# A transformer block in split fp32: mixing rebuilt in source order and overlapped with its neighbours, the MLP's first token block prepared inside it, masks as products in the scores' own type

## The chip, the cores and the metric

The kernel runs on one core of one Trainium2 chip. The metric is device microseconds of one launch, as a median over runs. Engines are named as in the profile: PE multiplies, PEld loads its weights, DVE, ACT and POOL work on vectors, SP issues the DMAs. Of the kernel before there are three runs: 1945.34, 1952.02 and 1945.75 us, median 1945.75.

## The reference

One sequence of S = 2048 tokens with D = 576 features, all fp32. `mod` is a vector of six modulations computed from a condition.

```
# attention: 32 heads of 18, causal window of 256
scores = where((0 <= i-j < 256), q @ k.T * 18**-0.5, -1e9);  o = softmax(scores) @ v
x = x + ga * (o @ wo)
h = layernorm(x) * (1 + cb) + sb
# mixing: four quarters of the features are shifted by +1, -1, +2, -2 tokens
u = gelu(layernorm(h) @ w1)
h1 = h + shift(u) @ w2
# MLP, F = 4608
out = x + gb * (h1 + gelu(layernorm(h1) @ w3) @ w4)
```

## The kernel before

**Arithmetic.** Each fp32 matrix is held as a high part in fp32r (a rounded fp32 that PE takes) and a low part, the rest. A product runs as three matmuls per 128 features: high·high, low·high, high·low. 576 features are four chunks of 128 and a tail of 64; the tail is stored twice in one chunk of 128 rows, high over low, so that one matmul makes two of its products. ACT casts the high part, DVE or POOL subtracts to get the low part. The w3 product is done by a Strassen scheme with seven products of half-size blocks (`OP`, `up` names P1 to P7); its operands on the activations' side are seven sums of quarter blocks, `A` (A11, A12, S3, ...), on the weights' side seven sums T1 to T4 and B11 to B22 of a slab of w3, `W`.

**Stages.** (1) `qkv`. (2) `attention`: 32 steps n, each of two head pairs j. Per j, four pairs of score blocks (`mx`, L522) of 64 queries against 320 keys, twice each, get the mask added by a second matmul with `identb` as weights and the mask `Mq` as moving operand (L524, or L526 where only one edge lies in the block). DVE takes row maxima (L534). Then the transposed scores X are computed in five banks of 512 columns (L566), with the masks `Mk` added by further matmuls (L591, nine per j), and ACT takes the exponential (L596). `identb`, `Mq` and `Mk` are bf16, the scores fp32r. Then P·V (L618), normalisation and a store of o to DRAM (`od`). Output tiles `wotile`: load o rows (`or`), transpose (`pa`, `pb`, L682/L684), split into T (L691 and before), 2 × 14 matmuls with Wo (L703), residual and layernorms, stores of x, h and the normalised h (`xp`, `hbd`, `xnd`). Tiles 12 to 15 run after the last heads.

(3) Mixing, `phase_b`: 8 groups of 256 tokens. Load `xnd`, transpose (L1055/L1057), split into T (L912/L913); five w1 chains per group (`pg`, L957, 14 matmuls of 256 columns, the last with the tail's 64 rows); gelu; high and low of the result into G (L961/L962, the tail chunk by quarters in L974/L975); small DVE copies carry the halo of one or two tokens between groups (L967 to L983), one right behind each chain's G; then per tile two chains with w2 (`w`, L1010, 14 matmuls of 288 columns). POOL makes `rr` = gb·h1 + x (L1020, L1021); SP stores it (`rd`) and the normalised h1 (`xmd`). w1 and w2 are loaded and split just before (`load_w1`, `load_w2`).

(4) MLP, `phase_m`: two token blocks of 1024, each 18 steps. Step jj uses slab j of w3 (256 of the 4608 columns) and w4. `wprep` loads a slab into the one buffer `wf` (L1089, L1090), sums on POOL (L1101), casts on ACT (L1107), splits on POOL (L1113) and DVE (the tail, L1121); for w4 POOL multiplies by gb (L1127) and splits (L1139). `up` is 7 × 7 matmuls of 512 columns (u0P, u1P, ..., L1211), combined, gelu, split into G (L1241); `down` is 16 × 6 matmuls of 288 (d, L1264), added by DVE to `acc` (L1272), which starts from `rd`. The A operands of a token block are made by `aprep`: load `xmd` into `rows` (L1159, L1160; the same buffer as `wf`), sums on POOL (L1167 to L1172), 84 transposes (L1182, L1183), splits (L1190 to L1192). The downs of step jj run between the products of step jj + 1, except around a block's end: there the last two downs run side by side with `aprep` of the next block.

**What sets the order.** `phase_a` (stages 1 and 2) collects events with hand-written nominal times (`tm(h)`, 11.5 a step) and plays them sorted. `phase_b` and `phase_m` play their own lists through a heap (`play`, `spread`), phase_b under the framework's own scheduling, phase_m in written order. Each has its own SBUF pools and PSUM pool; a pool's space passes to the next when the pool closes. Within an engine instructions run strictly in order.

Of the kernel before, what the change touches and what calls it, by code (L numbers as in the profile page):

```python
# [32 lines left out]
def spread(steps, t0, t1):  # L33
    n = len(steps)
    return [(t0 + (t1 - t0) * (k + 0.5) / n, f) for k, f in enumerate(steps)]


def play(timed):
    heap = [(t, n, f) for n, (t, f) in enumerate(timed)]
    heapq.heapify(heap)  # L40
    n = len(heap)
    while heap:
        f = heapq.heappop(heap)[2]
        for t, e in f() or ():
            heapq.heappush(heap, (t, n, e))
            n += 1


class Kern:
# [8 lines left out]
    def pool(self, stack, name, bufs=1, space=None):  # L58
        kw = {} if space is None else {"space": space}
        return stack.enter_context(self.tc.tile_pool(name=name, bufs=bufs, **kw))  # L60

    def split9(self, row, L, cs, name):
        nc = self.nc
        pa = self.ps.tile([P, KC, P], F32, tag="tr", name=name + "pa", bufs=self.b_tr)
        for k in range(KC):
            nc.tensor.transpose(pa[:, k, :], row[:, k * P:(k + 1) * P], self.ident)
        nc.scalar.copy(L[:, 0:KC, cs], pa)
        nc.vector.tensor_tensor(out=L[:, KC:2 * KC, cs], in0=pa, in1=L[:, 0:KC, cs].bitcast(F32), op=ALU.subtract)
        pb = self.ps.tile([TAIL, P], F32, tag="tr", name=name + "pb", bufs=self.b_tr)
        nc.tensor.transpose(pb, row[:, KC * P:D], self.ident)  # L70
        nc.scalar.copy(L[:TAIL, 2 * KC, cs], pb)
        nc.vector.tensor_tensor(out=L[TAIL:, 2 * KC, cs], in0=pb, in1=L[:TAIL, 2 * KC, cs].bitcast(F32), op=ALU.subtract)

    def passes(self, hi, lo):
        p = []
        for k in range(KC):
            p += [(hi[:, k, :], (slice(None), k)), (hi[:, k, :], (slice(None), KC + k)), (lo[:, k, :], (slice(None), k))]
        p.append((hi[:, KC, :], (slice(None), 2 * KC)))
        p.append((lo[:TAIL, KC, :], (slice(0, TAIL), 2 * KC)))
        return p  # L80

    def load_dup(self, raw, src):
        self.nc.sync.dma_start(raw[:TAIL], src)
        self.nc.sync.dma_start(raw[TAIL:], src)

    def stats(self, x, name):
        nc, sm = self.nc, self.sm
        st = sm.tile([P, 2, 6], F32, tag="bst", name=name + "st", bufs=3)
        mv = sm.tile([P, 2], F32, tag="bmv", name=name + "mv", bufs=4)
        rs = sm.tile([P, 1], F32, tag="brs", name=name + "rs", bufs=4)  # L90
        nc.vector.bn_stats(st[:, 0], x[:, 0:288])
        nc.vector.bn_stats(st[:, 1], x[:, 288:576])
        nc.vector.bn_aggr(mv, st)
        nc.gpsimd.tensor_scalar(rs, mv[:, 1:2], EPS, None, op0=ALU.add)
        nc.gpsimd.tensor_tensor(out=rs, in0=rs, in1=self.mhalf, op=ALU.pow)
        return mv[:, 0:1], rs

    def modulate(self, h, x, m, rs, scale_b, shift_b, way):
        nc = self.nc
        if way == "p":  # L100
            nc.vector.tensor_scalar(h, x, m, rs, op0=ALU.subtract, op1=ALU.mult)
            nc.gpsimd.tensor_tensor(out=h, in0=h, in1=scale_b, op=ALU.mult)
            nc.gpsimd.tensor_tensor(out=h, in0=h, in1=shift_b, op=ALU.add)
            return
# [60 lines left out]
    def masks(self):  # L165
        nc = self.nc
        g = nc.gpsimd
        for M in (self.Mq, self.Mk):
            g.memset(M, 0.0)
# [1182 lines left out]
```

## Time and profile before

| what | value |
|---|---|
| median of 3 runs | 1945.75 us |
| profiled execution | 1945.12 us |
| its span in the trace | 1943.1 us |
| mean granted clock of PE | 0.950 |
| instructions | 34458 |
| PE busy | 1763.9 us, 91% of the span |
| DVE / POOL / ACT busy | 1129.3 / 881.8 / 703.0 us |

The span runs from the first to the last instruction in the trace. Stages by the trace: qkv to about 230, attention to about 745, the last output tiles to 790, mixing to 959, the MLP from there (u0 first at 1014.5), its second token block from about 1437. Groups in the profile are named by line, engine and operation, `out<-in`, shapes, count; then busy time, mean ns of one, and the idle time of the engine just before them with what ended it.

### The profile page before, as it was taken

To read this page: it belongs to the slowest core of one execution; us is meant where nothing else is said; L and a number is where in the kernel's file an instruction comes from. 1 tells how busy PE (TensorE), PEld (TensorE's weight loads), DVE (VectorE), ACT (ScalarE), POOL (GpSimd) and SP (SyncE) were. 2 spreads that over 40 slices of the span, in tenths; PEclk is the share of its full clock that TensorE was granted. 3 is DMA by queue.
4 is the path that set the end of the run, shared out by engine and by line. 5 is a ranking of instruction groups with operands and counts; after the bars stand their busy time and mean duration, and the time that the engine had idled before them with its cause. 6 is when DMAs were issued, how large, how long until landed. Compare 5 with 4: busy or idle time off the path is not lost.

```text
span 1943.1 us, 34458 instructions
## 1 busy us (share of the span) xinstructions
PE 1763.9 (91%) x13752; PEld 1555.5 (80%) x13752; DVE 1129.3 (58%) x1943; ACT 703.0 (36%) x1225; POOL 881.8 (45%) x812
## 2 busy tenths in 40 slices
PE   7999978989989997699647999999988999999998
PEld 6788866778777776599636999999977899999997
DVE  3544335556565644567456666666666666666664
ACT  2222124444444443434133433333333333333331
POOL 4311354344534331133456655665543655555560
PEclk9999959899999998899869999999989999999999
DMA  4855443444544426434442111111114221211211
GB/s 141 305 173 179 162 135 86 124 129 118 168 129 146 127 85 192 156 134 136 134 125 69 58 58 58 58 58 57 58 49 127 66 62 57 60 58 58 65 47 49
DMA packets 157847, 206.68 MB, mean 106 GB/s; under 512 B 17140, under 2 KB 92532, under 8 KB 157112
## 3 DMA queue, kind: packets, MB, share of 16 engines
q1 hardware_dynamic: 157688, 204.49, 34.0%
q8 instruction: 108, 1.77, 0.4%
q14 instruction: 51, 0.42, 0.1%
HBM read 143.46 MB, written 60.56 MB: 105 GB/s over the span
## 4 chain that ended last, share of the span: by engine, by line
PE 40%; DVE 5%; POOL 2%; issue 2%; ACT 2%; DMA 1%; SPq 1%; DVEq 0%; POOLq 0%
PE d L1264 22%; DVE W L1121 2%; DVE G L1241 1%; DVE U L1217 1%; DMA wf<-in_B_w_dram 1%; ACT G L1234 1%; PE u33P L1211 1%; PE u23P L1211 1%; PE u9P L1211 1%; PE u8P L1211 1%; PE u30P L1211 1%; PE u25P L1211 1%; PE u22P L1211 1%; PE u13P L1211 1%; PE u11P L1211 1%
## 5 line engine op out<-in xcount | busy, mean ns | idle before, releaser
L1264 PE MATMUL d<-W,G 128*128 128x288 f32 x3456 | 510.4, 298 | 12.3 <-DVE acc L1272 10.6
L1264 PEld LDWEIGHTS d<-W,G 128*128 128x128 f32 x3456 | 490.5, 190 | 34.5 <-DVE acc L1272 12.2
L1272 DVE TENSOR_TENSOR acc<-d,acc 128x576 f32<-128x576 f32 x288 | 216.5, 753 | 189.8 <-PE d L1264 187.7
L1101 POOL TENSOR_TENSOR wf<-wf 128x384 f32<-128x384 f32 x140 | 147.4, 1074 | 358.3 <-DMA wf<-in_B_w_dram 358.3
L534 DVE TENSOR_REDUCE m<-mx 128x2 f32<-128x640 f32 x224 | 181.2, 817 | 168.6 <-PE mx L524 165.7
L596 ACT ACTIVATE P<-X 128x512 f32<-128x512 f32 (+4 forms) x320 | 179.6, 573 | 205.4 <-PE X L591 202.9
L522 PE MATMUL mx<-KD,QS 128*128 128x320 f32 (+4 forms) x512 | 175.6, 403 | 42.0 <-POOL QS L505 24.5
L566 PE MATMUL X<-QD,KS 128*128 128x64 f32 (+2 forms) x704 | 160.7, 323 | 4.8 <-ACT P L596 4.6
L505 POOL TENSOR_SCALAR QS<-QD,rowm 128x512 fp32r<-128x512 f32 x128 | 87.8, 699 | 163.6 <-DMA QD<-qd 61.3
L1241 DVE TENSOR_TENSOR G<-U,G 128x512 fp32r<-128x512 f32 x108 | 98.6, 913 | 97.5 <-ACT G L1234 97.4
L1113 POOL TENSOR_TENSOR W<-wf,W 128x768 fp32r<-128x768 f32 x70 | 152.0, 2193 | 0.0
L522 PEld LDWEIGHTS mx<-KD,QS 128*128 128x128 f32 x512 | 106.6, 210 | 48.8 <-POOL QS L505 30.2
L1232 ACT ACTIVATE U<-U 128x512 f32<-128x512 f32 x108 | 68.3, 632 | 181.0 <-DVE U L1217 181.0
L1232 ACT ACTIVATE C<-C 128x512 f32<-128x512 f32 x36 | 22.8, 632 | 286.6 <-DVE C L1217 286.6
L352 PE MATMUL qk<-hT,Wqk 128*128 128x512 f32 x504 | 120.8, 400 | 0.0
L566 PEld LDWEIGHTS X<-QD,KS 128*128 128x128 f32 x704 | 111.8, 203 | 7.5 <-ACT P L596 6.3
L352 PEld LDWEIGHTS qk<-hT,Wqk 128*128 128x128 f32 x504 | 95.8, 191 | 24.6 <-issue 1.4
L1107 ACT CAST W<-wf 128x1152 fp32r<-128x1152 f32 x70 | 90.6, 1321 | 66.2 <-DMA wf<-in_B_w_dram 52.2
L512 POOL TENSOR_SCALAR KS<-KD,rowm 128x768 fp32r<-128x768 f32 (+1 forms) x128 | 107.6, 854 | 0.6 <-PE v L382 0.6
L1139 POOL TENSOR_TENSOR W<-wf,W 128x1152 fp32r<-128x1152 f32 x35 | 96.2, 2749 | 22.8 <-ACT W L1133 22.8
L1127 POOL TENSOR_TENSOR wf<-wf,gbm 128x1152 f32<-128x1152 f32 x35 | 100.8, 2880 | 12.3 <-DVE acc L1272 12.3
L524 PE MATMUL mx<-Mq,identb 128*128 128x128 bf16 x448 | 106.0, 237 | 0.0
(888 smaller groups left out, 3189.8 us busy)
## 6 DMA issues: line engine op xcount, KB each, us to landing
wf<-in_B_w_dram SPq DMA_DIRECT2D x35, 576.0 KB
wf<-in_B_w_dram SPq DMA_DIRECT2D x140, 128.0 KB
KD<-kd SPq DMA_DIRECT2D x72, 216.0 KB
QD<-qd SPq DMA_DIRECT2D x96, 144.0 KB
wf<-in_B_w_dram SPq DMA_DIRECT2D x140, 64.0 KB
qd<-qs SPq DMA_DIRECT2D x16, 512.0 KB
kd<-qs SPq DMA_DIRECT2D x16, 512.0 KB
vd<-Vst SPq DMA_DIRECT2D x16, 312.0 KB
```

Of the source, the lines that this page charges most:

```text
L352: nc.tensor.matmul(po, W[:, a, fs], H[:, c, :], start=(n == 0), stop=(n == 13))
L512: nc.gpsimd.tensor_scalar(t[:, b0:, r], src[:, b0:], M[:, 2 + r:3 + r], 0.0, op0=ALU.mult, op1=ALU.add)
L522: nc.tensor.matmul(pm[:, s, 320 - 64 * nb:320], lhs, K[:, j, 64 * (i + 5 - nb):64 * (i + 5)], start=True, stop=False)
L534: nc.vector.tensor_reduce(out=m[:, c:c + 2], in_=pm[:, :, 0:320], axis=mybir.AxisListType.X, op=ALU.max, negate=True)
L566: nc.tensor.matmul(px[:, c:c + q1 - q0], K[:, b + 4].rearrange("p r k -> p (r k)"), Q[:, j, q0:q1], start=(i == 0), stop=False)
L596: nc.scalar.activation(p[:, lo:], X["px", n, j, k][:, lo:], AF.Exp, scale=SCALE)
L1101: nc.gpsimd.tensor_tensor(out=WF[:, o], in0=WF[:, a], in1=WF[:, b], op=ALU.subtract)
L1113: eng.tensor_tensor(out=W[:, s0:s1, 3:5, :], in0=WF[:, 1 + s0:1 + s1, 0:2], in1=W[:, s0:s1, 0:2, :].bitcast(F32), op=ALU.subtract)
L1211: nc.tensor.matmul(po, W[:, w - 1, a, :], X[:, b, :], start=(m == 0), stop=(m == 6))
L1241: nc.vector.tensor_tensor(out=G[:, 1, ta, b], in0=up_b[jj, "gf", ta, b], in1=G[:, 0, ta, b].bitcast(F32), op=ALU.subtract)
L1264: nc.tensor.matmul(po, G[:, g, ta, b, ts], W[:, w, b, cs], start=(n == 0), stop=(n == 5))
L1272: nc.vector.tensor_tensor(out=a, in0=po, in1=a, op=ALU.add)
```

## The change

Four parts. **Masks:** `identb`, `Mq` and `Mk` become fp32r (`identr`), so a mask matmul is of the same kind as the score matmul it adds to. **One list:** `phase_a`, `phase_bc`, `phase_b` and `phase_m` give way to one `build`, which collects the events of all stages in one list by nominal time (13.0 a step in attention, 17.7 a mixing group, 24.2 an MLP step) and plays it in written order, with one PSUM pool for the whole program and SBUF pools that hand over tile by tile.

**Mixing** is written anew in `mixing` and `mix_events`: w1 and w2 are loaded and split while the last Wo tiles run, with the low parts on POOL instead of DVE; T and the weights have the tail doubled, so every matmul has 128 rows; a group's halo copies stand together behind its last w1 chain; the first w1 chains stand between the last Wo tiles.

**MLP:** the A operands of the first token block are prepared inside mixing, their 84 transposes between the w1 and w2 chains around groups 4 to 6 (loaded from `xmd` of tiles 0 to 7). Slab 0 of w3 is placed where w1 and T lay, as soon as the last w1 chain is done. The tail's fourfold copy is a tile of its own (`dup`). At the switch of token blocks rows are loaded and summed earlier (during u17), the two downs are spread wider (0.72 instead of 0.53 of a step), and the transposes come in four packets between them.

On PE after the output tiles, the order before (rows of the last Wo tile, then mixing):

```order
L682 MATMUL pa_9757<-ident,or_9673 128x128 x4
L684 MATMUL pb_9762<-ident,or_9673 128x128
L703 MATMUL wo_0_9770<-Wo,T_9764 128x288 x14
L703 MATMUL wo_1_9788<-Wo,T_9764 128x288 x14
L1055 MATMUL xnT0pa<-ident,xn_10041 128x128 x4
L1057 MATMUL xnT0pb<-ident,xn_10041 64x128
L1055 MATMUL xnT1pa<-ident,xn_10043 128x128 x4
L1057 MATMUL xnT1pb<-ident,xn_10043 64x128
L957 MATMUL pg_4_10074<-T,W1a 128x256
```

and of the change, from Wo tile 14 (`ptm` are mixing's transposes):

```order
L786 MATMUL ptm_9829<-ident,xmr_9758 128x128 x4
L787 MATMUL ptm_9829<-ident,xmr_9758 128x128
L629 MATMUL wo_0_9840<-Wo,T_9820 128x288 x14
L807 MATMUL pg_4_9857<-xT_9551,W_9550 128x256 x14
L629 MATMUL wo_1_9873<-Wo,T_9820 128x288 x14
L807 MATMUL pg_0_9891<-xT_9551,W_9550 128x256 x14
L807 MATMUL pg_1_9933<-xT_9551,W_9550 128x256 x14
L608 MATMUL pa_9952<-ident,or_9792 128x128 x4
L610 MATMUL pb_9957<-ident,or_9792 128x128
L807 MATMUL pg_2_9973<-xT_9551,W_9550 128x256 x14
L629 MATMUL wo_0_9993<-Wo,T_9968 128x288 x14
```

The first group's w1 chains moved from behind Wo tile 15 to between the halves of tiles 14 and 15. On PE at the end of mixing, before:

```order
L1010 MATMUL w_1_11962<-W2m,G_11625 128x288 x12
L1010 MATMUL w_1_11962<-W2t,G_11625 128x288 x2
L1182 MATMUL pt_0_0_12074<-ident,rows_12066 128x128 x2
L1183 MATMUL pt_0_0_12074<-ident,rows_12066 128x128
L1182 MATMUL pt_0_1_12081<-ident,rows_12066 128x128 x2
L1183 MATMUL pt_0_1_12081<-ident,rows_12066 128x128
```

and of the change:

```order
L807 MATMUL pg_3_11895<-xT_9552,W_9550 128x256 x14
L856 MATMUL w_13_0_11949<-W_9547,Gm_9548 128x288 x14
L856 MATMUL w_13_1_11964<-W_9547,Gm_9548 128x288 x14
L856 MATMUL w_14_0_11986<-W_9547,Gm_9549 128x288 x14
L856 MATMUL w_14_1_12016<-W_9547,Gm_9549 128x288 x14
L856 MATMUL w_15_0_12038<-W_9547,Gm_9549 128x288 x14
L856 MATMUL w_15_1_12065<-W_9547,Gm_9549 128x288 x14
L1082 MATMUL u0P_12118<-A_10339,W_0_11918 128x512 x7
```

The transposes are gone from this place (they stand some groups earlier), and the first up-step follows mixing directly. On POOL at the same place, of the change (`rr` is mixing's residual, `wf` a raw slab, `W_0` slab 0 split, 3 and 4 of its 7 parts):

```order
L974 TENSOR_TENSOR wf_11924<-wf_11924 128x384 x4
L119 TENSOR_SCALAR d13rs<-d13mv 128x1
L120 TENSOR_TENSOR d13rs<-d13rs,mhalf 128x1
L869 TENSOR_TENSOR rr_12013<-x_13_11871,gb 128x576
L870 TENSOR_TENSOR rr_12013<-rr_12013,xpr_11893 128x576
L986 TENSOR_TENSOR W_0_11918<-wf_11924,W_0_11918 128x3x256
L119 TENSOR_SCALAR d14rs<-d14mv 128x1
L120 TENSOR_TENSOR d14rs<-d14rs,mhalf 128x1
L869 TENSOR_TENSOR rr_12061<-x_14_11933,gb 128x576
L870 TENSOR_TENSOR rr_12061<-rr_12061,xpr_11947 128x576
L986 TENSOR_TENSOR W_0_11918<-wf_11924,W_0_11918 128x4x256
```

Before, POOL had all of mixing's rows ahead of slab 0; now slab 0's sums and splits stand between those of tiles 13, 14 and 15. On SP the loads of slab 0 stand behind the store of tile 12's `rd` and those of slab 1 behind the stores of tiles 13 to 15.

The diff, cut to its core:

```diff
-        self.identb = c.tile([P, P], BF16, name="identb")
+        self.identr = c.tile([P, P], F32R, name="identr")
-        self.Mq = c.tile([P, 2, 64], BF16, name="Mq")
-        self.Mk = c.tile([P, 2, 64], BF16, name="Mk")
+        self.Mq = c.tile([P, 2, 64], F32R, name="Mq")
+        self.Mk = c.tile([P, 2, 64], F32R, name="Mk")
...
-                nc.tensor.matmul(o, self.identb, mv, start=False, stop=(i == len(ops) - 1))
+                nc.tensor.matmul(o, self.identr, mv, start=False, stop=(i == len(ops) - 1))
...
+    def mixing(self, T0, TB):
...
+        def w1split(k):
...
+            tt = nc.gpsimd.tensor_tensor
+            tt(out=m3(lo)[r], in0=v[r, :, 0:P], in1=m3(hi)[r].bitcast(F32), op=ALU.subtract)
...
+        def tev(t):
+            T, pt = X["T"][t // 2 % 2], X["pt", t]
...
+            nc.scalar.copy(T[:, 0:4, cs], pa)
+            nc.scalar.copy(T[:, 8, cs], pb)
+            nc.vector.tensor_tensor(out=T[:, 4:8, cs], in0=pa, in1=T[:, 0:4, cs].bitcast(F32), op=ALU.subtract)
+            nc.vector.tensor_tensor(out=T[:, 9, cs], in0=pb, in1=T[:, 8, cs].bitcast(F32), op=ALU.subtract)
...
+        def halo(g):
+            G = X["G"][g % 2]
+            cpy = nc.vector.tensor_copy
+            if g:
+                G0 = X["G"][(g - 1) % 2]
+                cpy(G[:, :, 0:4:2, 0:2], G0[:, :, 0:4:2, 256:258])
+                cpy(G0[:, :, 1:4:2, 258:260], G[:, :, 1:4:2, 2:4])
+                cpy(G[0:32, :, KC, 2:3], G0[0:32, :, KC, 258:259])
+                cpy(G0[32:64, :, KC, 257:258], G[32:64, :, KC, 1:2])
+                cpy(G[64:96, :, KC, 2:4], G0[64:96, :, KC, 258:260])
+                cpy(G0[96:128, :, KC, 256:258], G[96:128, :, KC, 0:2])
...
+    def mix_events(self, T1, TB, fns):
...
+        for g in range(NG):
+            s = T1 + TB * g
+            for n, fc in enumerate((4, 0, 1, 2, 3)):
+                at(s + 1.7 * n, w1mm, g, fc)
+                at(s + 1.7 * n + 1.8, w1ev, g, fc)
+            at(s + 1.7 * 5 + 1.1, halo, g)
+            if g + 1 < NG:
+                for i in range(2):
+                    tile_in(2 * g + 2 + i, s + 8.5 + .6 * i)
+            if g:
+                tile_out(2 * g - 1, s + 9.8)
+            tile_out(2 * g, s + 13.7)
...
+    def mlp_events(self, T1, Tc, T0, U, fns):
...
+        for i, tl in enumerate((61, 75, 86, 97)):
+            pair(0, i, T1 + tl, T1 + tl + 3, T1 + tl + 9, 9.0)
+        at(Tc + .02, begin2)
+        add(wprep(0, 0, None, Tc + .1, 18.0))
+        at(T0 - .02, begin3)
+        add(wprep(1, 1, 0, T0 - .01, 12.0))
...
+                d = 0.72 if sb + 1 < SB else 0.53
+                add(down(jj - 1, sb, t + 0.47 * U, d * U, False))
+                add(down(jj, sb, t + (0.47 + d) * U, d * U, True))
+                if sb + 1 < SB:
+                    for i in range(4):
+                        tl = 0.15 + 0.02 * i if i < 2 else 0.5 + 0.35 * (i - 1)
+                        ts = 0.3 if i == 0 else 0.18 + 0.35 * i
+                        pair(1, i, t + tl * U, t + ts * U, t + (0.5 + 0.35 * i) * U, 0.3 * U)
...
+                    add(wprep(jj + 2, js[-2], None, t + 1.9 * U, 0.55 * U))
...
+    def build(self):
+        tc = self.tc
+        with tc.manual_schedule():
+            HU = 13.0
...
+            te, wotile = self.attention(t1, t2, t1 + 6.0, HU)
...
+            for i in range(4):
+                wotile(12 + i, 35.45 + 0.6 * i)
+            mixf = self.mixing(te + .01, 17.7)
+            T1 = te + 30.0
+            Tc, T0 = self.mix_events(T1, 17.7, mixf)
+            self.at(T1 + 30.0, self.close, "wo")
+            mf = self.mlp()
...
+            self.at(Tc + .01, self.close, "mixa")
+            self.at(T0 - .03, self.close, "mixb")
+            self.mlp_events(T1, Tc, T0, 24.2, mf)
```

643 lines of the change are left out of this document (249 added, 394 removed).

## The prediction

> **What bounds the kernel now.** I read the page first, then busy time by windows, then TensorE's groups with the idle time ahead of them in the stretches where it is not busy, then the chain of waits there. In the page's slices PE is near full except at two dips, and the clock row dips with it.
>
> ```profile
> PE   7999978989989997699647999999988999999998
> PEclk9999959899999998899869999999989999999999
> ```
>
> The windows put times on them (columns: window, length, busy time of PE, weight loads, DVE, ACT, POOL; then granted clock, DMA share, GB/s).
>
> ```profile
> 240.00:740.00 500.00, 447.99 (x5783) 372.05 (x5790) 268.24 (x475) 216.09 (x420) 220.47 (x312) 0.91 0.43 124
> 780.00:800.00 20.00, 6.59 (x34) 5.90 (x34) 12.84 (x35) 5.41 (x12) 5.73 (x13) 0.75 0.57 183
> 820.00:940.00 120.00, 119.42 (x866) 110.21 (x866) 82.02 (x248) 44.92 (x121) 42.63 (x46) 1.00 0.41 137
> 960.00:980.00 20.00, 0.00 (x0) 0.00 (x0) 2.19 (x5) 2.52 (x2) 10.31 (x12) 0.60 0.34 113
> 1080.00:1420.00 340.00, 339.76 (x2051) 309.86 (x2050) 221.77 (x299) 128.71 (x170) 195.31 (x113) 1.00 0.20 58
> 1430.00:1450.00 20.00, 11.08 (x52) 9.17 (x50) 9.31 (x14) 7.84 (x13) 8.54 (x9) 0.80 0.19 59
> ```
>
> TensorE is the bound in the body of mixing (820 to 940) and of the MLP (1080 to 1420). What the change can win lies at the seams: attention to mixing (780 to 800), mixing to MLP (from 960) and between the MLP's token blocks (around 1440). From PE's groups between 958 and 1066 the one with most idle time ahead of it, and from the timeline how the third up-step begins:
>
> ```profile
> L1182 PE MATMUL pt<-ident,rows 128*128 128x128 f32 x56 | 14.1, 344 | 33.9 <-DMA rows<-xmd 29.5 <-ACT A L1190 2.0 <-DVE A L1192 1.8
> ```
>
> ```profile
> 1065.52 1.77 PE L1211 MATMUL u2P<-A,W 128*128 128x512 f32 x7
> ```
>
> I use that start of u2, 1065.5, as the mark: from there both kernels run the same steady MLP until u17. PE is done with mixing before the window at 960, so 106 us lie between, in which it needs 35 for u0, u1 and the downs of u0: 11.3 for a u step alone (the u18P row further down), and 24.0 for a u step with downs, which is 145 matmuls at the pace of the window of 2051 in 340 us. The chain of waits says why (start, length, what):
>
> ```profile
> 965.75 0.58 POOL d15rs L95
> ...
> 971.86 3.68 DMA wf<-in_B_w_dram
> ...
> 981.32 3.15 DVE W L1121
> ...
> 985.17 4.14 DMA rows<-xmd
> ...
> 1014.06 0.60 SPq L1090
> ```
>
> POOL's last statistics, then the whole preparation of W3 slab 0, then (rows share its buffer) the A operands, then slab 1.
>
> **Masks.** One pair of score and mask matmuls of the maxima, and one bank of X with two masks:
>
> ```profile
> 504.35 0.23 PE L524 MATMUL mx<-Mq,identb 128*128 128x128 bf16 x1
> 504.39 0.39 PE L522 MATMUL mx<-KD,QS 128*128 128x320 f32 x1
> 504.62 0.23 PE L524 MATMUL mx<-Mq,identb 128*128 128x128 bf16 x1
> ```
>
> ```profile
> 500.62 0.57 PE L566 MATMUL X<-QD,KS 128*128 128x64 f32 x3
> ...
> 501.12 0.39 PE L522 MATMUL mx<-KD,QS 128*128 128x320 f32 x1
> ```
>
> ```profile
> L522 PEld LDWEIGHTS mx<-KD,QS 128*128 128x128 f32 x490 | 102.3, 210 | 45.7 <-POOL QS L505 28.0 <-DVE m L534 8.2 <-issue 4.0
> ...
> L524 PEld LDWEIGHTS <-identb 128*128 128x128 bf16 x438 | 43.3, 99 | 31.8
> ```
>
> A pair takes 504.62 − 504.35 = 0.27 us, most of it from the score's start to the mask's, so part of a weight load is already not hidden. A mask in f32r brings an f32 load (210 ns, not 99). The transposes below start 0.43/4 = 0.108 us apart; I price a mask at that, and the 320-column product at 320/288 of a w2 row below (0.14), 0.155: a pair is 0.263, 0.01 less, times 512 −5 us. The bank takes 501.12 − 500.62 = 0.50 now; with two short pieces and two masks at 0.108 and one long at 0.155 it is 0.59, +0.09. Over five banks, most with fewer short pieces, I put +0.3 us per head pair, times 64 = +19. Net +14 of PE work; PE has gaps in attention (448 of 500 us busy by the windows), and I let them take half: **+7**. Bounds: if every load hides, pairs at 0.22 and banks as now, 512 × 0.05 = −26; all on the path, +14.
>
> The rule that speaks against this edit is in the Trainium skill, TensorE: Matmul & The Clock Gate, section on weight-path perf modes: fast weight load is on with 128 weights and an input type that is not FP32. The trace agrees in kind: 99 ns for bf16 weights, 210 ns for f32. Taken alone, with no load hidden, it makes this edit cost what rival 3 works out from those two rows, against +7 here; the overlap seen above (0.27 for a pair whose busy times add to 0.62) speaks for the smaller price.
>
> **Mixing.** The body's rows:
>
> ```profile
> 845.00 0.60 PE L1055 MATMUL xnT7pa<-ident,xn 128*128 128x128 f32 x4
> ...
> 845.46 1.66 PE L957 MATMUL pg<-T,W1m 128*128 128x256 f32 x12
> 846.96 0.59 PE L957 MATMUL pg<-T,W1t 128*128 128x256 f32 x2
> 847.48 1.85 PE L1010 MATMUL w<-W2m,G 128*128 128x288 f32 x12
> 849.17 0.43 PE L1010 MATMUL w<-W2t,G 128*128 128x288 f32 x2
> 849.44 0.28 PE L957 MATMUL pg<-T,W1a 128*128 128x256 f32 x1
> ```
>
> The wait at the start of the stage, and two DVE groups in its body:
>
> ```profile
> L1055 PE MATMUL xnT1pa<-ident,xn 128*128 128x128 f32 x4 | 1.1, 435 | 9.8 <-DVE T L913 9.8
> ```
>
> ```profile
> L962 DVE TENSOR_TENSOR G<-gf,G 128x256 fp32r<-128x256 f32 x32 | 13.4, 419 | 4.1 <-ACT G L961 3.8
> ...
> L913 DVE TENSOR_TENSOR T<-xnT2pa,T 128x512 fp32r<-128x512 f32 x1 | 0.7, 693 | 0.0
> ```
>
> Twelve w1 matmuls take 1.50 us (845.46 to 846.96), the last two 0.52, because the last has 64 rows; in the new code all fourteen are whole: 1.75 instead of 2.02, and 40 such chains save 11 us. A w2 chain takes 1.96 (847.48 to 849.44). New body: 40 × 1.75 + 32 × 1.96 + (80 + 84) transposes × 0.108 = 70 + 63 + 18 = 150 us, the 84 being the first token block's, now in here. New stalls: the halo copies come in one batch behind a group's last w1 chain and ahead of the odd tile's w2. Behind that chain DVE has two subtractions of T (0.69 each, and a small one behind each), one of G (0.42) and the six copies. With the activation and casts ahead of them I estimate 3.7 us, against 1.5 that PE has in ten transposes and the first three w2 matmuls: 2.2 us a group, times 7 = 15, and 4 more where DVE also splits A. Bounds: 0, if PE's other work covers them, and 19 more, if A's splits fall into the gap each time. The start: before, PE stood idle 9.8 us for T, and only then came the transposes and the first w1 chain. In the new order w1 chains stand between the last Wo tiles; I keep the Wo tiles' own waits (they run from od's stores and loads, which are unchanged) and count PE dense from 778, when tile 15 begins: 778 + 7 (masks) + 4 (tile 15) + 150 − 5 (chains done in the earlier gaps) + 19 = **953 for the end of mixing**, with the A operands ready; before it was 959 without them.
>
> **First MLP steps.** POOL's queue decides here.
>
> ```profile
> L1101 POOL TENSOR_TENSOR wf<-wf 128x384 f32<-128x384 f32 x8 | 7.8, 999 | 20.4 <-DMA wf<-in_B_w_dram 20.4
> L1020 POOL TENSOR_TENSOR rr<-x,gb 128x576 f32<-128x576 f32 x5 | 7.2, 1439 | 16.4 <-DVE x L1011 16.4
> ```
>
> ```profile
> 1027.55 5.85 POOL L1113 TENSOR_TENSOR W<-wf,W 128x768 fp32r<-128x768 f32 x2
> 1033.35 2.65 POOL L1139 TENSOR_TENSOR W<-wf,W 128x1152 fp32r<-128x1152 f32 x1
> ```
>
> Let p be the end of the last w1 chain, 953 minus six w2 chains (11.8), so 941. Slab 0's loads stand on SP behind tile 12's stores and go out near p. Data at p + 7.5, four sums of 1.0 to p + 11.5; then POOL's order puts one tile's statistics and rr work (0.8 + 2 × 1.44 = 3.7) ahead of each of the two W splits (about 2 and 3 of the 5.85 that both take): p + 17 and p + 24. The first product of u0 needs the first split, the second the second: u0's last six sevenths run to p + 24 + 9.7, which is 975. Slab 1's loads stand on SP behind the stores of tiles 13 to 15, and rr of tile 15 is behind slab 0's splits on POOL: issue at p + 27.5. From its first issue (some 0.6 before 1014.06) the old slab 1 took 1033.4 − 1013.4 = 20 us to the end of the W split and 22.6 to that of W4: u1's first product at about p + 45, the first down at p + 50. From there 24 − 1.6 us of PE work lead to u2: 941 + 50 + 22.4 = 1013. **u2 at 1013, −52.5.** Bounds: as if queues were free, 988 (rival 1); and 10 us later, if u2's slab, which waits for the same buffer, is late once more.
>
> **Switch of token blocks.**
>
> ```profile
> L1211 PE MATMUL u19P<-A,W 128*128 128x512 f32 x49 | 14.9, 441 | 7.0 <-DVE W L1121 3.4 <-POOL W L1113 3.0 <-ACT W L1107 0.6
> L1182 PE MATMUL pt<-ident,rows 128*128 128x128 f32 x56 | 11.4, 287 | 4.4 <-DMA rows<-xmd 4.4
> L1183 PE MATMUL pt<-ident,rows 128*128 128x128 f32 x28 | 8.1, 288 | 4.5 <-POOL rows L1172 4.5
> L1211 PE MATMUL u18P<-A,W 128*128 128x512 f32 x49 | 11.3, 389 | 0.0
> ```
>
> The 4.4 and 4.5 go, since rows are loaded and summed during u17; the clock behind them, 0.80 over the 20 us from 1430, cost up to 4, of which I take 3.6. The next slab is loaded no earlier relative to u19 (rows hold its buffer until the last transpose), so its 7.0 stay. **−12.5.** The end of the program is unchanged.
>
> Sum against the profiled execution, 1945.1 (span 1943.1, and 2 us around it): 1945.1 − 52.5 − 12.5 = 1880.1. The masks' +7 and the earlier end of mixing are in the −52.5. The median of the runs, 1945.75, is 0.6 above that execution, within their spread: **1880**.
>
> **Rivals.** (1) The two queues bind less: POOL reaches both splits by p + 13 and SP's stores drain early, so u0 and u1 run dense behind mixing: u2 at 953 + 35 = 988, −77.5; half of u19's 7.0 goes too, −16 at the switch: 1852; if the masks' loads hide as well (−26 in place of +7), 1819. For it: POOL is busy only 43 of 120 us in mixing. Against: one buffer holds a slab. (2) DVE becomes the bound of mixing: 82 of 120 us busy now, and halo, A and T splits cluster; 3 us more in each of eight groups (24), and the tail subtractions of the first two slabs (3.15 and more in the chain above) behind it, some 8: 1880 + 32 = 1912. (3) The f32 weight loads of the masks don't hide at all: 210 − 99 = 111 ns on each of 64 × (8 + 9) = 1088 masks is +121 in place of +7, 1994, slower than before. It decides from (65 + 7)/1088 = 66 ns a mask. For it: masks stand alone between products with loads of their own. Against: in the bank of 0.50 us three f32 loads of some 0.2 have room. (4) The new waits eat everything: slab 1 waits as long as before and u2 comes at 1060: 1940, no change.
>
> **How the numbers follow.** Forecast 55%, (1) 20%, (2) 18%, (3) 4%, (4) 3%. The forecast's own bounds: 33 less to 7 more on masks, 19 less to 19 more on halo stalls, 25 less to 10 more on the first slabs; not all at one end. The range 1826 to 1914 takes in (1) but for its far end, and (2), and leaves out (3) and (4). A measurement tells 0.5%, 10 us, from no change. Faster 0.93, same 0.03, slower 0.04.
>
> **What would show it.** Right: one idle gap of about 10 us ahead of u1, released by POOL's W split; PE above 95% busy from 800 to 950; halo gaps released by DVE copies; mask rows some 0.11 apart. Wrong: u2 before 995 or after 1030; attention longer or shorter by over 15 us; a first w1 chain later than 785.

## The result, and the profile after

The changed kernel takes 1925.99 us in the median of four runs (1922.91 to 1928.77), against 1948.35 for the kernel before in the four runs it now has; the ratio is 0.9884, with a 95% interval from 0.9858 to 0.991. The profiled execution took 1925.45 us (span 1923.7), 19.7 less than that of before. The forecast was 1880: the sign is right, and two thirds of the gain did not come.

Marks read from the timelines of the two profiled executions, in us from the span's start:

| mark | before | forecast | after |
|---|---|---|---|
| last score matmul of attention | 711 | 718 | 707 |
| end of mixing on PE | 959 | 953 | 986 |
| u0 starts | 1014.5 | 958 | 985.6 |
| u2 starts | 1065.5 | 1013 | 1052.5 |
| u20 starts | 1531.7 | 1467 | 1516.2 |
| end of the span | 1943.1 | 1878 | 1923.7 |

Up to u2 39.5 us are missing, behind it 6. The page's slices of PE, and its clock:

```profile
PE   7999998989999996787767999999998999999998
PEclk9999958899999998998887999999998999999999
```

The one deep dip of before (a slice of 4) is gone, but in its place a shallow one is several slices wide. By windows, in the same columns as before:

```profile
820.00:940.00 120.00, 97.47 (x697) 93.83 (x696) 78.04 (x179) 38.49 (x97) 53.58 (x60) 0.91 0.41 134
...
1000.00:1020.00 20.00, 6.94 (x23) 4.45 (x21) 7.64 (x4) 4.85 (x5) 14.07 (x8) 0.65 0.56 184
...
1080.00:1400.00 320.00, 320.00 (x1939) 292.59 (x1938) 206.17 (x279) 122.82 (x160) 190.05 (x109) 1.00 0.19 57
```

From 820 to 940, where PE was busy for 119.42 of 120 us, it is now busy for 97.47 at a clock of 0.91. DVE and POOL aren't full there either (78 and 54 of 120). PE's groups between 735 and 986 say what it waits for:

```profile
L856 PE MATMUL w<-W,Gm 128*128 128x288 f32 x448 | 69.8, 314 | 16.8 <-DVE Gm L830 10.6 <-DVE x L860 3.5 <-DVE xr L633 1.5
L629 PE MATMUL wo<-Wo,T 128*128 128x288 f32 x140 | 23.1, 327 | 11.1 <-DVE T L617 11.1
L1063 PE MATMUL pt<-ident,rows 128*128 128x128 f32 x56 | 11.9, 300 | 7.5 <-issue 5.2 <-DVE A L1073 1.3 <-ACT A L1071 1.1
...
L1064 PE MATMUL pt<-ident,dup 128*128 128x128 f32 x28 | 8.5, 305 | 7.0 <-POOL dup L1053 7.0
```

The halo copies (L830) cost 10.6 us, near the forecast's 15. The preparation's own waits (ahead of the rows' and dup's transposes) are 14.5 where 4 were allowed; 5.2 of them are "issue", for which the profile names no releaser. The clock, 1.00 from 820 to 860, is 0.91 in the 40 us from 860 and 0.83 in the 40 from 900, where these gaps (up to 3.3 us) lie. In the first MLP steps (985 to 1053):

```profile
L1082 PE MATMUL u1P<-A,W 128*128 128x512 f32 x49 | 17.0, 490 | 14.4 <-POOL W L986 5.4 <-DVE W L994 4.6 <-ACT W L980 4.4
...
L1082 PE MATMUL u0P<-A,W 128*128 128x512 f32 x49 | 13.1, 428 | 5.0 <-POOL W L986 5.0
```

And at the switch of token blocks (1410 to 1518): the waits for rows are smaller (2.1 for a bank, 2.6 for dup), while the wait of u19 stayed, 6.0 for 7.0, and that for DVE's sums into `acc` grew from 1.0 to 3.2.

```profile
L1135 PE MATMUL d<-W,G 128*128 128x288 f32 x302 | 52.0, 316 | 4.5 <-DVE acc L1143 3.2 <-ACT G L1105 1.2
L1082 PE MATMUL u19P<-A,W 128*128 128x512 f32 x49 | 15.4, 454 | 6.0 <-POOL W L986 3.1 <-DVE W L994 2.9
...
L1063 PE MATMUL pt<-ident,rows 128*128 128x128 f32 x56 | 10.9, 278 | 2.1 <-DVE U L1088 2.1
L1064 PE MATMUL pt<-ident,dup 128*128 128x128 f32 x28 | 8.0, 285 | 2.6 <-POOL dup L1053 2.6
```

### The profile page after: what moved, and what is told of

Its sections match the earlier page's. It is cut to its first block, busy times and chain, and to the rows that moved or that the text cites. A ratio compares the mean times of both kernels' runs of the same rounds, so it can differ in the third digit from the quotient of the medians.

```text
span 1923.7 us, 34258 instructions
## 1 busy us (share of the span) xinstructions
PE 1766.7 (92%) x13752; PEld 1617.1 (84%) x13752; DVE 1124.2 (58%) x1840; ACT 697.9 (36%) x1194; POOL 899.6 (47%) x831
## 4 chain that ended last, share of the span: by engine, by line
PE 57%; DVE 8%; DMA 3%; POOL 3%; ACT 3%; issue 3%; SPq 1%; DVEq 0%; POOLq 0%; ACTq 0%
PE d L1135 23%; PE av L544 3%; PE wo L629 3%; PE mx L448 2%; PE X L492 2%; PE w L856 2%; PE pg L807 1%; DVE W L994 1%; PE X L517 1%; DVE G L1112 1%; DMA wf<-in_B_w_dram 1%; PE mx L450 1%; PE u33P L1082 1%; PE u32P L1082 1%; PE u26P L1082 1%
## 5 line engine op out<-in xcount | busy, mean ns | idle before, releaser
L1135 PE MATMUL d<-W,G 128*128 128x288 f32 x3456 | 510.2, 298 | 12.5 <-DVE acc L1143 10.0
L448 PE MATMUL mx<-KD,QS 128*128 128x320 f32 (+4 forms) x512 | 168.5, 379 | 28.0 <-POOL QS L431 14.0
L492 PE MATMUL X<-QD,KS 128*128 128x64 f32 (+2 forms) x704 | 156.2, 313 | 1.2 <-ACT P L522 0.7
L1112 DVE TENSOR_TENSOR G<-U,G 128x512 fp32r<-128x512 f32 x108 | 94.4, 874 | 99.0 <-ACT G L1105 99.0
L517 PE MATMUL X<-Mk,identr 128*128 128x128 f32 (+1 forms) x576 | 112.3, 269 | 0.0
L1000 POOL TENSOR_TENSOR wf<-wf,gb 128x1152 f32<-128x1152 f32 x35 | 103.1, 2946 | 13.1 <-DMA wf<-in_B_w_dram 6.9
```

Of the source, the lines that this page charges most:

```text
L448: nc.tensor.matmul(pm[:, s, 320 - 64 * nb:320], lhs, K[:, j, 64 * (i + 5 - nb):64 * (i + 5)], start=True, stop=False)
L492: nc.tensor.matmul(px[:, c:c + q1 - q0], K[:, b + 4].rearrange("p r k -> p (r k)"), Q[:, j, q0:q1], start=(i == 0), stop=False)
L517: nc.tensor.matmul(o, self.identr, mv, start=False, stop=(i == len(ops) - 1))
L1112: nc.vector.tensor_tensor(out=G[:, 1, ta, b], in0=up_b[jj, "gf", ta, b], in1=G[:, 0, ta, b].bitcast(F32), op=ALU.subtract)
L1135: nc.tensor.matmul(po, G[:, g, ta, b, ts], W[:, w, b, cs], start=(n == 0), stop=(n == 5))
```

## The experiments

All start from the changed kernel unless another is named. The theory: waits come from the order in which the in-order queues are filled, and go when one thing is moved. The rival: a wait that is removed comes back on the next queue, since each piece passes SP, POOL, ACT and DVE in turn. The edits are cut to their core; `...` marks lines left out.

**Masks.** One run takes the masks back to bf16 in the changed kernel, the other puts f32r masks alone into the kernel before.

```diff
-        self.identr = c.tile([P, P], F32R, name="identr")
+        self.identr = c.tile([P, P], BF16, name="identr")
...
-        self.Mq = c.tile([P, 2, 64], F32R, name="Mq")
+        self.Mq = c.tile([P, 2, 64], BF16, name="Mq")
...
```

> The changed kernel with the masks and the identity back in bf16, all else as changed. My price of the prediction (+7 us for f32r masks): about 1919 us, attention (first score to last P.V) 7 us shorter. Rival, from the two traces, in which attention takes the same time before and after: a mask's own f32 load costs what the explicit bf16 load and the gap behind it cost, so within 3 us of the changed kernel's 1926. Third: f32r masks are the gain (pairs 0.256 against 0.274 us), then bf16 is some 5 to 10 us slower, 1931 to 1936.

> The kernel before with the masks and their identity in f32r, nothing else: one part of the change alone. After the run with bf16 masks in the changed kernel (1916 against 1926) the theory is that an f32r mask costs about 10 ns more each, 1088 of them, and a little in the early attention steps: 8 to 14 us slower than before (ratio 1.004 to 1.007). Rival, that the loss came only with the new order of the Wo work around it: within 4 us of before (ratio 0.998 to 1.002).

1916.01 us with bf16 masks, 10 less than the changed kernel; 1956.29 with f32r masks alone, a ratio of 1.0041 to before (1.0019 to 1.0062), 8 us. Both are near the forecast's +7. In the timeline of the changed kernel a bank of three X pieces and two masks now lasts from 501.65 to 502.28:

```profile
501.65 0.57 PE L492 MATMUL X<-QD,KS 128*128 128x64 f32 x3
502.05 0.39 PE L517 MATMUL X<-Mk,identr 128*128 128x128 f32 x2
502.28 0.36 PE L448 MATMUL mx<-KD,QS 128*128 128x320 f32 x1
502.48 0.22 PE L450 MATMUL mx<-Mq,identr 128*128 128x128 f32 x1
502.53 0.36 PE L448 MATMUL mx<-KD,QS 128*128 128x320 f32 x1
```

0.63 us against 0.50: +0.13 where +0.09 was forecast. That attention nevertheless is no longer than before has another cause: with bf16 masks its last score matmul stands at 693, against 711 before. Between 430 and 705 PE's idle time ahead of the score matmuls fell from 17.0 us (before) to 7.7 (changed kernel):

```profile
L522 PE MATMUL mx<-KD,QS 128*128 128x320 f32 x278 | 93.5, 395 | 17.0 <-DVE m L534 7.5 <-POOL QS L505 3.6 <-DMA or<-od 2.8
```

```profile
L448 PE MATMUL mx<-KD,QS 128*128 128x320 f32 x282 | 88.7, 366 | 7.7 <-DVE m L460 3.4 <-POOL c6rs L119 0.6 <-POOL c8rs L119 0.6
```

So the new order is worth about as much in attention as the masks cost; which shift in it does this wasn't tried. The two later pairs that differ in the masks put their price lower: 5.5 us from e2 to e11, and 8.7 from e9 to e14.

**One wait of mixing at a time.** Halo copies ahead of the T splits on DVE (e2); dup ahead of rr on POOL (e3); two buffers for the x rows that SP waits for (e4); sums and dup off POOL (e6).

```diff
# e2
-            at(s + .3, tev, t)
+            at(s + .35, tev, t)
...
-            at(s + 1.7 * 5 + 1.1, halo, g)
+            at(s + 8.65, halo, g)
# e3
-            at(tt - 1.6, adup(sb, i))
+            at(tt - (4.0 if sb == 0 else 1.6), adup(sb, i))
# e4 (room from the statistics' buffers, 2 for 3)
...
-            r = X["xp", t] = mb([P, D], F32, tag="xp", name=f"xpr{t}", bufs=1)
+            r = X["xp", t] = mb([P, D], F32, tag="xp", name=f"xpr{t}", bufs=2)
# e6
-                    tt = nc.gpsimd.tensor_tensor
+                    tt = nc.gpsimd.tensor_tensor if sb else nc.vector.tensor_tensor
...
-                    nc.gpsimd.tensor_copy(d, r[:, :, 256:288].unsqueeze(2).to_broadcast([P, 7, 4, 32]))
+                    (nc.gpsimd.tensor_copy if sb else nc.scalar.copy)(d, r[:, :, 256:288].unsqueeze(2).to_broadcast([P, 7, 4, 32]))
```

> The changed kernel with a group's halo copies moved ahead of the next tiles' T subtractions on DVE; nothing else moves. Theory that queue order makes the waits: the 10.6 us that w2 waits for DVE's halo copies fall below 3, mixing ends about 8 us earlier, total about 1918. Rival, that DVE and ACT are the bound there and a wait removed comes back one place later (the T operands of the next group late instead): under 3 us gained, 1923 or more, with the idle time ahead of the next group's w1 or its transposes.

> The changed kernel with the copy of the tail rows (dup, POOL) put ahead of a tile's rr products on POOL in the first token block's preparation. Queue-order theory: PE's 7.0 us of waits for dup go, and with them part of the half clock that follows the 3.3 us gaps (clock 0.69 to 0.86 in the 10 us windows behind them), so mixing ends 8 to 12 us earlier, total 1914 to 1918. Rival (POOL late in any order): rr moves behind, SP's stores and loads behind rr are later, gain under 3 us.

> The changed kernel with two buffers in place of one for the x rows that rr needs (xpr), so SP's load of the next tile's rows doesn't wait for POOL's rr of the last; room for it from two statistics buffers in place of three. In the changed kernel SP waits 93 us in mixing on that line, up to 20 at a time, with all later loads and stores behind it. Theory that SP's queue is the late one: mixing's operand loads and slab 0 come earlier, the end of mixing 5 to 10 us earlier and u1's slab too, total 1910 to 1920. Rival, that SP has slack and the waits on POOL and DVE order stand by themselves: under 3 us, 1923 to 1927.

> The changed kernel with the first token block's four sums of rows on DVE and the copy of the tail (dup) on ACT, instead of both on POOL; the second block as changed. Moving dup alone gained nothing, since the sums ahead of it stayed behind rr on POOL and the splits of A behind. Theory that POOL's in-order queue makes PE wait in groups 4 to 6 (7.0 us for dup, 5.2 put down to issue, and the half clock behind them): both waits under 2 us, mixing ends 10 to 15 us earlier, total 1911 to 1916. Rival, that DVE is the bound in those groups: the sums' 3 us each delay halo and A splits there, gain under 4 us, total 1922 or more.

e2 1913.9, e3 1925.91, e4 1926.77, e6 1928.45. Only the halo order paid, 12 us in the medians. The two profiled executions differ by 14: 9 in mixing (from the last Wo matmul to the last w2 matmul 177.8 us against 186.8), 4 ahead of it and 3 from u0 to u2, with 1.5 lost behind. The 4 come from attention, which the edit does not touch: from the first to the last score matmul it takes between 472.1 and 480.7 us in the twelve profiles of the changed kernel's order with f32r masks, so a few us of any total here are spread. In e2's groups the wait is gone:

```profile
L856 PE MATMUL w<-W,Gm 128*128 128x288 f32 x448 | 67.1, 307 | 6.8 <-DVE x L860 3.5 <-DVE xr L633 1.5 <-DVE Gm L829 1.2
```

In e3 the 7.0 for dup fell to 0.2, and those of the rows' transposes rose from 7.5 to 11.1; in e6 the wait for dup is 0.0 and DVE's A splits take 9.4:

```profile
L1063 PE MATMUL pt<-ident,rows 128*128 128x128 f32 x56 | 11.8, 296 | 11.1 <-issue 5.1 <-DVE A L1073 4.3 <-ACT A L1071 1.7
...
L1064 PE MATMUL pt<-ident,dup 128*128 128x128 f32 x28 | 8.3, 296 | 0.2 <-POOL dup L1053 0.2
```

```profile
L1063 PE MATMUL pt<-ident,rows 128*128 128x128 f32 x56 | 11.7, 295 | 11.7 <-DVE A L1073 9.4 <-issue 2.4
```

e4 is the plainest case. SP's waits in mixing by line, in the changed kernel and in e4:

```profile
SPq L864 <- POOL rr L870: 52.7, 4, 19.7
SPq L864 <- DMA xpr<-xp: 19.0, 7, 4.1
```

```profile
SPq L878 <- DVE xm L875: 92.6, 8, 19.7
```

The queue waits longer, for the store of xm that stands next in it. For these three the rival holds.

**The whole preparation a slot earlier** (e9, on e2): loads, sums and dup together.

```diff
-            at(tt - 1.6, adup(sb, i))
+            at(tt - (4.0 if sb == 0 else 1.6), adup(sb, i))
...
-        for i, tl in enumerate((61, 75, 86, 97)):
-            pair(0, i, T1 + tl, T1 + tl + 3, T1 + tl + 9, 9.0)
+        for i, (tl, tt) in enumerate(((58, 70), (71.5, 84), (79, 95), (93, 106))):
+            pair(0, i, T1 + tl, T1 + tl + 3, T1 + tt, 9.0)
```

> The kernel of e2 (halo copies first) with the first token block's preparation a slot earlier on all its queues at once: the loads of rows on SP ahead of the x rows and stores they stood behind, the sums on POOL right behind them, dup right behind the sums; the transposes' places stay. Moving dup alone, or the sums off POOL alone, only moved the wait (to A's splits, to DVE behind a late load). Theory that the first of the queues, SP, hands its lateness on: PE's waits for rows, dup and A's splits in groups 4 to 6 (about 18 us in e2) fall under 6, the clock in the window from 860 to 940 rises over 0.95 from 0.88, mixing ends 12 to 18 us earlier, total 1897 to 1904. Rival, that POOL or DVE is full in these groups: the waits come back at halo copies, w1 or the next rr, total 1910 or more.

1911.3: 3 us beside e2. Mixing is 5.6 shorter, and dup's wait is 0, but rows' transposes still wait 14.2, half of it without a named releaser. The forecast of 12 to 18 fails.

```profile
L1063 PE MATMUL pt<-ident,rows 128*128 128x128 f32 x56 | 11.6, 294 | 14.2 <-issue 7.4 <-DVE A L1073 5.8 <-ACT A L1071 1.1
```

**The preparation behind mixing**, where the kernel before has it (e13).

```diff
-        for i, tl in enumerate((61, 75, 86, 97)):
-            pair(0, i, T1 + tl, T1 + tl + 3, T1 + tl + 9, 9.0)
+        T0 += 28.5
+        for i in range(4):
+            tt = Tc + 21.5 + 6.5 * i
+            tl = Tc + 13.0 + .1 * i if i < 2 else tt - 8.0
+            pair(0, i, tl, tl + 3.5, tt, 5.0)
```

> The changed kernel with the first token block's preparation taken out of mixing and put behind slab 0, between mixing and u0, where the kernel before has it; everything else as changed. Theory that putting it inside mixing gave back what it saved: mixing ends 20 to 28 us earlier (its waits for dup, rows and A, their half clock and 9 us of transposes gone), the preparation then costs as much behind it, total 1920 to 1932. Rival, that the move was worth what the prediction counted (25 us of preparation for 9 of transposes): 1938 or more.

1936.8 in ten runs (1926.8 to 1941.95). Mixing ends at 957 in place of 986, 28.6 us earlier, and u2 starts at 1068.6 in place of 1052.5, 16 later. So the preparation cost mixing 28.6 us (31 from the last Wo matmul, which stands 2.4 later in e13): 9 are the forecast's price of its transposes, 14.5 the waits ahead of them shown above, and the rest goes with the lower clock, 0.83 against e13's 0.96 from 900 to 940. The move is worth 11 in the medians: between both expectations. Where it stands behind, its waits are longer:

```profile
L1063 PE MATMUL pt<-ident,rows 128*128 128x128 f32 x56 | 18.4, 432 | 23.4 <-ACT A L1071 12.1 <-DMA rows<-xmd 11.4
...
L1064 PE MATMUL pt<-ident,dup 128*128 128x128 f32 x28 | 11.8, 423 | 9.7 <-POOL dup L1053 9.7
```

**The first slabs.** e7 puts slab 0's splits and slab 1's loads, casts and tail ahead of the last tiles' work; e10 (on e2) does so on POOL and SP alone; e12 (on e2) fills PE's waits in u0 and u1 with matmuls of zeros.

```diff
# e7
-        add(wprep(0, 0, None, Tc + .1, 18.0))
+        add(wprep(0, 0, None, Tc + .1, 8.0))
-        add(wprep(1, 1, 0, T0 - .01, 12.0))
+        e1 = wprep(1, 1, 0, Tc + 11.5, 12.0)
+        at(Tc + 5.0, e1[0][1])
+        add(e1[1:-2])
...
# e10
...
+        for n, tn in ((5, 4.9), (7, 5.0), (6, 5.2), (9, 5.4)):
+            e0[n] = (Tc + tn, e0[n][1])
...
+        e1[0] = (Tc + 5.0, e1[0][1])
# e12
+                    fill = {(0, 1): 18, (1, 0): 16, (1, 1): 20, (1, 6): 17} if key == "P1" else {}
...
+                                nc.tensor.matmul(pw[:, 0], self.zb, self.zb.unsqueeze(1).to_broadcast([P, 4, P]), start=True, stop=True)
```

> The changed kernel with slab 0's splits ahead of tiles 13 to 15's rr on POOL, and slab 1's loads ahead of those tiles' stores on SP (its sums still behind their rr on POOL); the W4 part as before. Theory that queue order at the first MLP steps is what holds u1: u0 starts right behind mixing without its 5.0 us wait, slab 1's data are there some 10 us earlier, so u2 comes 10 to 18 us earlier relative to the end of mixing (67 us now), total 1908 to 1916. Rival, that the slab's own chain of load, sums, casts and splits sets it: u1 as late as now, 60 to 67 us, total 1920 or more.

> The kernel of e2 with slab 0's splits ahead of tiles 13 to 15's rr on POOL and slab 1's loads ahead of those tiles' stores on SP, while ACT's casts and DVE's tail subtractions of both slabs keep their places (in e7 ACT's casts of slab 1 stood ahead of the copy of u0's first product, 15.5 us, and DVE's tail ahead of a residual, 11.0). Theory that queue order sets the start of the MLP: u0 starts without its 5 us wait, and from u0's start to u2's takes 50 to 56 us in place of 64 in e2, total 1900 to 1906. Rival, that the slabs' chain itself is as long as the wait: 62 us or more, total 1911 or more.

> The kernel of e2 with PE's waits inside the first products of u0 and u1 filled by matmuls of zeros into a bank that nobody reads (18, then 16, 20 and 17 of them), sized to end about when the awaited split does. No work is saved and no wait is shorter. Theory that the half clock behind these waits (0.50 from 1008 to 1024 and 0.84 to 1053 in the changed kernel) is a loss of its own: u1's rest runs at full clock, u2 comes 4 to 8 us earlier relative to the first wait, total 1906 to 1910. Rival, that the slabs' chain through the one buffer (issue to issue 23 us) sets u2 whatever PE's clock is: within 2 us of e2's 1914.

e7 1925.75, e10 1918.72, e12 1918.9. In e7 PE waits 11.0 us for a residual behind the tail's subtraction on DVE and 15.5 for a copy behind slab 1's casts on ACT:

```profile
L1082 PE MATMUL u0P<-A,W 128*128 128x512 f32 x49 | 13.9, 449 | 15.5 <-ACT U L1095 15.5
...
L856 PE MATMUL w<-W,Gm 128*128 128x288 f32 x50 | 8.6, 340 | 11.0 <-DVE x L860 11.0
```

From the start of the last w1 matmul to u2 it is 85.1 us in the changed kernel, 81.6 in e2, 82.2 in e12, and between 84 and 86.5 in every other run with the preparation inside mixing. What stays the same under all these orders is the stretch from the first load of slab 0 to the first down, 54.8 to 56.6 us; in it slabs 0 and 1 pass the one buffer. The timeline of SP in the changed kernel has the first load of slabs 0, 1, 2 and 3 at

```profile
967.95 0.39 SPq L962 DMA_DIRECT2D wf<-in_B_w_dram  x1
...
998.38 0.39 SPq L962 DMA_DIRECT2D wf<-in_B_w_dram  x1
...
1021.37 0.38 SPq L962 DMA_DIRECT2D wf<-in_B_w_dram  x1
...
1044.13 0.37 SPq L962 DMA_DIRECT2D wf<-in_B_w_dram  x1
```

that is 30.4, 23.0 and 22.8 us apart, while a steady MLP step takes 24.0. e10 shortened the first interval to 22.1 (963.26 to 985.38) and got 32.5 in the second, since the sums of slab 1 waited on POOL for the last tile's rr. A second buffer for a slab wasn't tried, so that the buffer sets the first down is borne out by these 55 to 57 us, not by a run that breaks it.

u2 itself does not wait for its slab. In the changed kernel slab 2's last split ends at 1044.05, 8 us ahead of u2, whose matmuls follow those ahead of them without a gap, as they do in every profile here. What is long between the first down (1023.4) and u2 (1052.5) is PE's own work at a mean clock of 0.83, and the 3.1 us that downs wait:

```profile
1038.72 5.33 DVE L994 TENSOR_TENSOR W<-wf,W 32x896 fp32r<-32x896 f32 x2
...
L1082 PE MATMUL u2P<-A,W 128*128 128x512 f32 x3 | 0.8, 389 | 0.0
...
1023.40:1052.50 29.10, 27.28 (x138) 24.47 (x139) 19.27 (x23) 10.54 (x14) 15.92 (x10) 0.83 0.30 89
```

e12 held the clock in the wait, but not behind it. The stretch from u1's first product to the first down, from there to u2, and the first 7 us of the latter, in e2 and in e12:

```profile
996.00:1011.30 15.30, 4.08 (x7) 2.06 (x7) 9.41 (x4) 4.94 (x6) 12.30 (x6) 0.50 0.35 130
1011.30:1036.80 25.50, 24.59 (x138) 22.31 (x139) 17.90 (x22) 9.87 (x13) 15.11 (x8) 0.92 0.24 69
...
1011.30:1018.00 6.70, 6.66 (x31) 6.08 (x31) 3.94 (x6) 2.99 (x5) 1.01 (x1) 0.71 0.62 180
```

```profile
999.80:1015.20 15.40, 10.48 (x45) 4.70 (x45) 9.49 (x5) 4.96 (x6) 12.34 (x6) 1.00 0.32 119
1015.20:1041.00 25.80, 24.56 (x139) 22.09 (x140) 18.06 (x22) 9.92 (x13) 15.07 (x8) 0.93 0.24 69
...
1015.20:1022.00 6.80, 6.60 (x31) 5.84 (x32) 3.90 (x6) 2.98 (x5) 1.01 (x1) 0.75 0.60 173
```

The clock in the wait is 1.00 in place of 0.50. Behind it the clock falls all the same, to 0.75 over the first 6.8 us against 0.71 in e2, and the 25.5 us there are 25.8. So nothing was gained, but neither does the run show what a full clock behind the wait would be worth: in the changed kernel PE ran at 0.51 over the 6.6 us behind the first down.

**The switch.** e8 draws the second block's transposes together (0.25 of a step apart); in it the sums of two packets stand ahead of their loads, so the second block's operands aren't the reference's. e15 has them behind (0.27 apart), and its edit is the one shown.

```diff
-                        tl = 0.15 + 0.02 * i if i < 2 else 0.5 + 0.35 * (i - 1)
-                        ts = 0.3 if i == 0 else 0.18 + 0.35 * i
-                        pair(1, i, t + tl * U, t + ts * U, t + (0.5 + 0.35 * i) * U, 0.3 * U)
+                        tl = 0.15 + 0.02 * i if i < 2 else 0.47 + 0.27 * (i - 1)
+                        ts = 0.3 + 0.1 * i if i < 2 else tl + 0.14
+                        pair(1, i, t + tl * U, t + ts * U, t + (0.5 + 0.27 * i) * U, 0.26 * U)
...
-                    add(wprep(jj + 2, js[-2], None, t + 1.9 * U, 0.55 * U))
+                    add(wprep(jj + 2, js[-2], None, t + 1.6 * U, 0.55 * U))
```

> The changed kernel with the second token block's four packets of transposes 0.25 of a step apart in place of 0.35, and slab 19's load at 1.52 in place of 1.9 steps, so that the one buffer is free earlier. Theory that the slab behind the rows holds u19: its wait of 6.0 us and the half clock behind it go, total 1917 to 1921, unless PE then waits for rows or splits of A by as much. Rival, that DVE's splits bound this stretch: idle before the transposes grows from 4.7 to over 9 us and the total stays within 3 us of 1926.

> The changed kernel with the second token block's packets of transposes 0.27 of a step apart in place of 0.35, each packet's sums behind its own load (in e8 the sums of two packets stood ahead of their loads), and slab 19's load at 1.6 in place of 1.9 steps. Theory that the one buffer, held by the rows until the last transpose, makes u19 wait: its 6.0 us go, u17's start to u20's falls from 104 us to under 99, total 1918 to 1922. Rival, that sums and loads of the tighter packets make the transposes wait as long: 104 or more, total 1924 to 1930.

1930.93 and 1929.14. In e15 u19 no longer waits, as the theory has it, and yet u17 to u20 takes 107.4 us in place of 104.2: u18 waits for ACT's copy behind slab 19's casts, and dup behind two packets' sums.

```profile
L1082 PE MATMUL u19P<-A,W 128*128 128x512 f32 x49 | 13.6, 420 | 0.0
L1082 PE MATMUL u18P<-A,W 128*128 128x512 f32 x49 | 13.3, 428 | 5.2 <-ACT U L1095 3.8 <-DVE U L1088 1.4
...
L1064 PE MATMUL pt<-ident,dup 128*128 128x128 f32 x28 | 8.3, 296 | 5.8 <-POOL dup L1053 5.8
```

**What adds.** e11 is e2 with bf16 masks, e14 that with e9's earlier preparation, e16 that with e15's switch.

> The kernel of e2 with bf16 masks: do the two gains add? The halo copies gave 12 us (9 in mixing) and bf16 masks 10, in different stages: 1902 to 1906 if they add; 1908 or more if the shorter attention only brings the mixing's other waits forward (in the run with bf16 masks alone 14 us of attention became 9 at the end).

> Halo copies first, preparation a slot earlier, bf16 masks: the version that should beat both. e11 with two of the three gave 1908, e9 took 5 us off mixing beside e2 and lost 3 behind it: 1900 to 1907 if they add, 1908 if the third only moves waits.

> e14 with the switch of e15: 1896 to 1899 if e15's theory holds, 1901 to 1905 if its rival does.

1908.38, 1902.6 and 1906.34 us. In e11 the two gains did not add in full: 5.5 us beside e2, where bf16 masks alone had brought 10. e14 has the lowest median: a ratio of 0.9779 to before (0.9759 to 0.9799), 23 us below the changed kernel. e16, with e15's switch on top, is 3.7 us above it, worse than either of its expectations.

## Why the prediction was wrong

The views were read rightly: the seams were where time could be won, and the long idle stretch from 959 to 988 went. The failing steps are terms of the sum, in order of size.

**Mixing's end, 953 forecast, 986 measured.** The step that failed is the price of the preparation inside mixing: 84 transposes of 0.108 us and 4 us of stalls, 13 in all. e13 shows 28.6. The trace had the durations, but I let POOL's sums, rr products and dup, SP's loads and DVE's splits lie beside each other, though each stands in a queue behind another tile's work. The runs that moved one of these waits (e3, e6, e9) bear that out, but of the waits left ahead of the rows' transposes there a fifth to a half have no named releaser, so not every link is shown.

The other 17 us are there without the preparation: mixing ended at 957 in e13, where the forecast has 940. The start was late. "PE dense from 778, when tile 15 begins" became tile 14 at 781, and no w1 chain was done in the earlier gaps: 4 us of Wo matmuls and the forecast's 5 us of chains more lay behind it. So the 11 us that attention's end stood ahead of the forecast (707 for 718) did not reach the Wo tiles, of which tile 12 waited 8.8 us for T (2.7 before):

```profile
759.73 5.70 PE L629 MATMUL wo<-Wo,T 128*128 128x288 f32 x28 [8.81 <-DVE T L617]
```

And w2 waits for residuals as well as for the halo copies, some 5.5 us that the sum put at nothing. In e13:

```profile
L856 PE MATMUL w<-W,Gm 128*128 128x288 f32 x448 | 70.1, 317 | 18.4 <-DVE Gm L830 11.8 <-DVE x L860 4.0 <-DVE xr L633 1.5
```

The halo stalls (15 forecast, 10.6 measured, 9 gained in mixing by e2) and the price of a w1 and a w2 chain held.

**First MLP steps.** With p the end of the last w1 chain (967.7), p + 72 was forecast for u2 and p + 85 measured. POOL's first split ended at p + 17 as forecast, and the second at p + 25 for p + 24. That u0 started at p + 18 is then partly chance: the six w2 chains ahead of it took 18 us in place of 11.8, so PE was free no earlier. The first down came at p + 56, 6 us later than forecast. From there "24 − 1.6 us of PE work", 22.4, became 29.1 (25.5 to 29.8 in the other runs with the preparation inside mixing): the step priced PE's work at full clock and without waits. Rival 1, free queues, is out: no order tried with the preparation inside mixing brought u2 nearer than 81.6 us to the last w1 matmul.

**The switch and the end.** −12.5 forecast for the switch, −1.4 measured from u17 to u20 (105.5 to 104.1 us). The rows' waits went from 8.9 to 4.7, not to 0, and the wait for DVE's sums into `acc` grew by 2. Another 3.9 us went behind u20, where the forecast had no change (411.3 to 407.4, and 406.7 to 408.6 in all runs on the changed kernel); this wasn't looked into. That the whole stretch from u2 to the end is only 6 us short of the forecast is in part this luck.

**Masks.** +7 forecast, 5.5 to 10 measured in four pairs of runs, inside the bounds; of the two prices weighed, the one with overlapped loads was right, and Rival 3's +121 is out. What the sum lacked is the gain of some 10 us that the new order brings in attention.

Rival 2 had the right kind of answer (mixing delayed by clustering halo, A and T work, 1912), but not its reason: DVE is busy for 78 of 120 us and POOL for 54. Neither is full; where a wait was removed, another took its place in three of four single moves. Of the prediction's own signs of being wrong, u2 after 1030 came (1052.5); attention's length and the first w1 chain (784.4) stayed inside theirs.

## What to carry to other kernels

A piece of work that is put into another stage to fill it costs what its whole chain of queues costs there, not what its matmuls take: follow each of its instructions to what stands ahead of it on its engine, the DMA queue first. Where a wait is removed, name the next queue that the piece passes before counting the gain; three of four single moves here gained nothing. And where the items of a start-up go one after another round one buffer, measure from the first load to the first matmul that stands behind the second item before moving single instructions: here that stretch kept its 55 to 57 us in every order that was tried.

## What the runs showed of the hardware

The masks' own loads took 201 to 245 ns on average in f32r and 99 to 112 in bf16, some 112 us more over the 1088 masks. The time grew by 5.5 to 10 us, under 10 ns a mask: more than nine tenths of the longer loads were hidden.

```profile
L450 PEld LDWEIGHTS mx<-Mq,identr 128*128 128x128 f32 x448 | 89.8, 201 | 0.0
```

The pair of score and mask even got shorter (0.27 before, from 504.35 to 504.62; 0.25 now, from 502.28 to 502.53), and the bank with short pieces got longer (0.50 to 0.63).

Matmuls of zeros that nobody reads held the granted clock at 1.00 through a wait of 15.4 us in which it was 0.50 without them. They did not keep it there: in the 6.8 us behind the wait it was 0.75, against 0.71 without them.
